# Values in front of the scores in the steady rounds of a window attention

## The chip, the cores and the metric

The kernel runs on one core of one Trainium2 chip. What counts is the time of one execution on the device in microseconds; the kernel before takes 2110.75 us, the median of three runs (2108.05 to 2111.23).

## What is computed

The input has 4 batches of 8 heads, 768 positions and a head dimension of 64. Each position attends to the 4 first positions of its sequence (the sinks) and to the 128 last ones (the window). The result, 3072 rows of 512, goes through 8 experts that are all applied, weighted by a gate that is normalised in 8 sweeps over rows and columns:

```python
keep = is_sink | in_window                 # n_sink = 4, window = 128
scores = np.where(keep, scale * q @ k.T, -1e9)
a = np.exp(scores - scores.max(-1)); a = a / (a.sum(-1) + 1e-09)
x = (a @ v)                                # rows of 8 heads x 64
logits = x @ w_gate                        # then exp, and 8 sweeps to P
out = sum(P[:, e:e+1] * (np.maximum(x @ w1[e], 0) @ w2[e]) for e in range(8))
```

## The kernel before

**Stages.** Attention comes first and takes the first 263 us of the span. The experts follow, in stages that are matmuls almost throughout. While attention runs, pieces of the first expert's products fill TensorE's time (`plain`, with the tiles g and o).

**Units and rounds.** A unit is one block of 128 queries of one batch and half of the heads (4 of 8): 4 batches x 6 blocks x 2 halves give 48 units, numbered n. The rounds are a software pipeline over the units. A steady round n (L868 to L935 in `steady_round`, n from 6 to 48) does, in the order of the code:

- it transposes queries and keys of unit n + 2 (L474 on VectorE, into KQ),
- it computes the scores of unit n + 1 (L502), one matmul for each of 4 heads, into the PSUM tiles st0 to st3,
- VectorE masks the scores and finds their extremes (L510), ScalarE takes the exponentials (L513): `soften`,
- it computes the values of unit n - 1 (L602): the attention weights PT times vr, and behind them the sinks' products (PS times VS),
- it does a piece of the expert's first product (L695) and one step of the gate's logits (L642),
- VectorE divides for unit n + 1 (L519, L520); ScalarE and VectorE finish the piece of the expert (L700, L701),
- TensorE transposes the weights of unit n (L543, into st1 and st2); VectorE copies one pair of heads to PT, ScalarE the other (both L549),
- `store_x` reads the values O of unit n - 1: ScalarE copies the share of a block that is begun (L619), VectorE adds the share that completes a block (L615),
- TensorE transposes the sinks' weights (L567, into st3), ScalarE copies them to PS (L569), and a piece of the expert's second product (L711) ends the round.

An attention window of 128 spans two blocks of keys, so the values of a unit go half to its own block and half to the one before; that is why a block is begun by one unit and completed by the next.

**What sets the order.** The steady rounds stand under a manual schedule: every engine issues in the order of the code. An engine takes its instructions in that order, and waits at one until the semaphores that it names have come.

**The tiles that matter.** O is the PSUM tile that the values write. It comes from a pool of two buffers that are taken in turn (`ps_o`), and the gate's logits (L640) are tiles of the same pool and name. So where a gate's tile was begun since the last O, the next O takes the buffer of the O just before it, which `store_x` read at the end of the last round. The tiles st0 to st3 serve scores, transposes and the sinks' transposes in turn.

Of the kernel before, what the change touches and what calls it, by code (L numbers as in the profile page):

```python
# [233 lines left out]
def tile_sink_attention_moe(ctx: ExitStack, tc: tile.TileContext, q, k, v, wg, w1, w2, out):  # L234

    nc = tc.nc
# [128 lines left out]
    def st_tile(shape, k=None):  # L365
        if k is None:
            k, turns[0] = turns[0] % 4, turns[0] + 1
        return ps_st.tile(shape, F32, name=f"st{k}")
# [96 lines left out]
    def transpose_qk(n):  # L465

        b, i, hh = units[n]
        us[n] = {}
        h0 = hh * HH
        t = KQ[hh]  # L470
        to = t[:, :, SINK:].rearrange("p r (a c) -> p r a c", a=2)[:, :, :, turn_of(b, i)]
        if n >= 2 * GB * FIRST:
            src = KS[n // (2 * GB)].rearrange("p (r a i t) -> p r a i t", r=HP, a=2, i=GB)[:, hh * NP:(hh + 1) * NP, :, i % GB]
            us[n]["high"] = nc.vector.transpose(to, src).ins  # L474
        else:
            pt = st_tile([P, 4, P], 3 if n == 1 else 0)
            for pr in range(NP):
                for j, nm in enumerate(("kr", "qr")):
                    nc.tensor.transpose(pt[:, 2 * pr + j, :], raws[nm, b, i][:, h0 + 2 * pr:h0 + 2 * pr + 2, :].rearrange("p h d -> p (h d)"), ident)
                    if n < 2 and (pr, j) in ((0, 0), (1, 1)) and (n, pr) != (0, 1):  # L480
                        spin(1, 5 - 2 * pr)
            us[n]["high"] = nc.scalar.copy(to, pt.rearrange("p (r a) t -> p r a t", a=2)).ins
        if i == 1:
            with nullcontext() if steady[0] else tc.issue_after(us[n]["high"]):
                nc.vector.tensor_copy(t[:, :, 0:SINK], t[:, :, place(b, 0)][:, :, 0:SINK])

    def scores(n, pr):

        b, i, hh = units[n]
        u = us[n]  # L490
        K, Q = KQ[hh][:, :, seen(b, i)], KQ[hh][:, :, CW:][:, :, turn_of(b, i)]
        if pr == 0:
            u["sc"] = att.tile([P, HH, CW], F32, name="sc", bufs=3)
            u["st"] = att.tile([P, 3, HH], F32, name="st", bufs=3)
            u["ps"] = {}
        hs = range(2 * pr, 2 * pr + 2)
        ps = {h: st_tile([P, K.shape[2]], h) for h in hs}
        u["ps"].update(ps)

        for h in hs:  # L500
            r0 = (h % 2) * D
            nc.tensor.matmul(ps[h], lhsT=Q[r0:r0 + D, pr, :], rhs=K[r0:r0 + D, pr, :], start=True, stop=True)  # L502
# [78 lines left out]
    def values(n):  # L581

        b, i, hh = units[n]
        u = us[n]
        keys, ready, _ = due_keys(n)
        if not keys:
            return
        O = u["O"] = ps_o.tile([P, NP, 2, P], F32, name="O")
        u["side"] = {q_: j for j, q_ in enumerate(sorted(keys[0][1], key=lambda q_: spot(keys[0][0], keys[0][1][q_])))}
        ops = []  # L590
        for pr in range(NP):
            for m, qs in keys:
                R = spots(PTR[hh][pr], [spot(m, s_) for s_ in qs.values()])
                sides = sorted(u["side"][q_] for q_ in qs)
                for h in range(2):
                    ops.append((O[h * D:(h + 1) * D, pr, sides[0]:sides[-1] + 1], raws[("vr", *units[m][:2])][:, hh * HH + 2 * pr + h, :], R[:, h]))
        for q_ in ready:
            if units[q_][1]:
                for pr in range(NP):
                    ops.append((O[:, pr, u["side"][q_]], seq[units[q_][0]][:, (hh * NP + pr) * P:(hh * NP + pr + 1) * P], us[q_]["PS"]))  # L600
        for j, (o_, x_, y_) in enumerate(ops):
            nc.tensor.matmul(o_, lhsT=x_, rhs=y_, start=(j < 2), stop=(j >= len(ops) - 2), skip_group_check=True)  # L602

    xrs = {}

# [196 lines left out]
    on = lambda j: 0 <= j < L  # L802
# [6 lines left out]
    def early_round(n):  # L809

        if units[n + 2][2] == 0:
            with (tc.high_priority() if n == -2 else nullcontext()):
                load_rows(("kr", "qr"), n // 2 + 1)
                if n < 2:
                    load_rows(("vr",), n // 2 + 1)
                elif n == 4:
                    load_rows(("vr",), n // 2)
            if units[n + 2][1] == 0:
                load_sinks(units[n + 2][0])
        squares_due(n)  # L820
        if n == -2:
            nc.sync.dma_start(wg_raw, wg.rearrange("(k p) e -> p k e", p=P))
            spread_sinks(0)
            split_sinks(0)
        if n == 0:
            spin(1, 4)
            scores(1, 0)
            soften(1, (0, 1))
            spin(1, 4)
            scores(1, 1)  # L830
            spin(1, 4)
            transpose_qk(2)
            with tc.issue_after(us[0]["divided"]), tc.issue_after(us[2]["high"]):
                soften(1, (2, 3))
            divide(1, range(HH))
        elif on(n + 1):
            for pr in range(NP):
                scores(n + 1, pr)
                soften(n + 1, range(2 * pr, 2 * pr + 2))
            divide(n + 1, range(HH))  # L840
        if on(n - 1):
            values(n - 1)
        if n >= START:
            run_fill(1)
        gate_step()
        for j in (0, 1) if n == -2 else (n + 2,) if n > 0 else ():
            transpose_qk(j)
        if on(n):
            transpose_p(n, 0)()
            if units[n][1]:  # L850
                gather_sinks(n)
        gate_step()
        if on(n):
            transpose_p(n, 1)()
        if on(n - 1):
            store_x(n - 1)
        gate_step()
        if on(n) and units[n][1]:
            transpose_sinks(n)
        if 0 < n < 3:  # L860
            spin(4 if n == 1 else 5, 5)
        if n >= START:
            run_fill(1)
# [4 lines left out]
    def steady_round(n):  # L868

        if n % 2 == 0:  # L870
            if on(n):
                load_rows(("vr",), n // 2)
            for j in (n // 2 + 1, n // 2 + 2) if n == STEADY else (n // 2 + 2,):
                if j < FIRST * GB:
                    load_rows(("kr", "qr"), j)
            if on(n + 2) and units[n + 2][1] == 0:
                load_sinks(units[n + 2][0])
        if n in ROWS:
            ROWS[n][0](ROWS[n][1])
        mid.extend(coming)  # L880
        coming.clear()
        behind[0] = False
        squares_due(n)
        turned = n + 2 < 2 * GB * FIRST
        if on(n + 2) and not turned:
            transpose_qk(n + 2)
        if on(n + 1):
            for pr in range(NP):
                scores(n + 1, pr)
        if on(n) and units[n][1]:  # L890
            gather_sinks(n)
        if on(n + 1):
            for h in range(HH):
                soften(n + 1, (h,))
        if on(n - 1):
            values(n - 1)
        run_fill(1)
        gate_step()
        flush(mid)
        behind[0] = True  # L900
        if on(n + 1):
            divide(n + 1, range(HH))
        flush(late)
        if turned:
            transpose_qk(n + 2)
        lows = [transpose_p(n, 0)] if on(n) else []
        gate_step()
        if on(n):
            lows.append(transpose_p(n, 1))
        flush(lows)  # L910
        if on(n - 1):
            store_x(n - 1)
        gate_step()
        if on(n) and units[n][1]:
            transpose_sinks(n)
        run_fill(1)
        flush(late)
        if n in PIECES:
            in_turn(*plain_tiles(*PIECES[n]))
        if n == L - 8:  # L920
            first_pieces.extend(pieces1(0))
        if n == L - 2:
            first_pieces.extend(pieces1(1))
        for _ in range({L - 8: 1, L - 6: 1, L - 4: 1, L - 3: 1, L - 2: 1, L - 1: 1, L: 2}.get(n, 0)):
            in_turn(*first_pieces.pop(0))
        flush(act_end)
        if on(n):
            b, i, hh = units[n]
            if (i, hh) == (0, 0):
                spread_sinks(b)  # L930
            elif (i, hh) == (0, 1):
                split_sinks(b)
        flush(pool_end)
        if L - 10 <= n < L - 2:
            sums1((n - (L - 10)) // 4, (n - (L - 10)) % 4)  # L935
# [785 lines left out]
```

## Time and profile before

| | |
|---|---|
| median of three runs | 2110.75 us |
| profiled execution | 2108.8 us |
| its span, first to last instruction | 2106.8 us |
| granted TensorE clock, mean | 0.999 |
| TensorE busy | 2087.2 us, 99% of the span |
| VectorE, ScalarE, GpSimd busy | 70%, 40%, 33% |
| steady rounds of attention | 37.8 to 263 us |

The times of the tables below count from the span's start. "PE" is TensorE's matmuls, "PEld" its weight loads, DVE is VectorE, ACT ScalarE. An fp32 matmul of the code stands in the trace as two, each with its weight load, so four scores are eight rows; and rows of one group that follow each other are merged, with their count behind an x. A matmul's end is modelled, so I go by the starts.

### The profile page before, as it was taken

What the parts mean: (1) busy time and instruction counts of PE and PEld (TensorE: products, weight loads), DVE (VectorE), ACT (ScalarE), POOL (GpSimd) and SP (SyncE); (2) the same over time, 40 slices, a digit from 0 to 9 for tenths busy, and PEclk for the clock granted to TensorE, in tenths of its full rate; (3) what the DMA queues carried; (4) which work ended last, traced back from release to release, by engine and by line L of the source; (5) the groups of instructions that cost most, each with busy time, mean ns of one, the idle gap of its engine ahead of it and who ended that gap; (6) DMA issues with size and microseconds to landing.
All of it is one profiled execution on the core that took longest, in us unless ns stands there. A gap on an engine that the chain in (4) does not pass through costs nothing.

```text
span 2106.8 us, 30678 instructions
## 1 busy us (share of the span) xinstructions
PE 2087.2 (99%) x10093; PEld 1708.5 (81%) x10093; DVE 1475.6 (70%) x2650; ACT 834.3 (40%) x1777; POOL 692.1 (33%) x854
## 2 busy tenths in 40 slices
PE   8999999999999999999999999999999999999998
PEld 6777778888888888888888888888888888888887
DVE  6777687777777766856766666666766666666666
ACT  6766625444444444433323233222433323233322
POOL 5654522233232331332232223223322232223223
PEclk9999999999999999999999999999999999999999
DMA  8656249989899996776666666668766666666662
GB/s 165 131 109 122 50 144 308 305 291 314 285 307 302 295 312 226 242 264 202 202 199 196 209 199 197 202 203 303 254 208 192 204 205 195 200 204 196 198 197 85
DMA packets 437269, 454.29 MB, mean 216 GB/s; under 512 B 139056, under 2 KB 305136, under 8 KB 436208
## 3 DMA queue, kind: packets, MB, share of 16 engines
q1 hardware_dynamic: 436184, 451.58, 69.4%
q8 instruction: 83, 1.36, 0.3%
q10 hardware_dynamic: 920, 0.68, 0.1%
q14 instruction: 82, 0.67, 0.1%
HBM read 314.69 MB, written 137.46 MB: 215 GB/s over the span
## 4 chain that ended last, share of the span: by engine, by line
PE 95%; DVE 1%; ACT 1%; DMA 1%; SPq 1%; POOL 1%; issue 0%; POOLq 0%; ACTq 0%; DVEq 0%
PE c L985 41%; PE o L1545 21%; PE held L1545 8%; PE o L1230 7%; PE held L1230 7%; PE O L602 2%; PE st L502 2%; PE st L543 2%; PE g L695 1%; PE o L711 1%; SPq L448 1%; PE O L642 1%; ACT sc L513 0%; DMA r<-in_moe_w_dram 0%; PE O L711 0%
## 5 line engine op out<-in xcount | busy, mean ns | idle before, releaser
L1011 ACT CAST hf<-w 128x512 fp32r<-128x512 f32 x448 | 265.1, 620 | 562.9 <-POOL w L1510 299.7
L1545 PE MATMUL o<-hf,W2q 128*128 128x512 f32 x1920 | 472.0, 389 | 0.0
L1545 PEld LDWEIGHTS o<-hf,W2q 128*128 128x128 f32 x1920 | 359.9, 188 | 75.5 <-DVE acc L1559 0.9
L985 PE MATMUL c<-T,W1q 128*128 128x512 f32 x1530 | 388.8, 389 | 0.2 <-DVE w L1491 0.2
L1012 DVE TENSOR_TENSOR hf<-w,hf 128x512 fp32r<-128x512 f32 x448 | 329.4, 764 | 76.3 <-ACT hf L1011 68.8
L985 PEld LDWEIGHTS c<-T,W1q 128*128 128x128 f32 x1530 | 286.8, 188 | 60.7 <-DVE w L1491 0.9
L1559 DVE TENSOR_TENSOR acc<-o,acc 128x512 f32<-128x512 f32 x298 | 204.7, 688 | 170.1 <-PE o L1545 170.0
L985 PE MATMUL c<-B,W1q 128*128 128x512 f32 x1134 | 278.3, 389 | 0.0
L985 PEld LDWEIGHTS c<-B,W1q 128*128 128x128 f32 x1134 | 212.6, 188 | 44.0
L1510 POOL TENSOR_TENSOR w<-w 128x512 f32<-128x512 f32 x64 | 82.6, 1291 | 493.2 <-DVE w L1492 493.2
L1491 DVE TENSOR_TENSOR w<-c,M 128x512 f32<-128x512 f32 x192 | 132.4, 689 | 137.9 <-PE c L985 133.6
L1487 ACT COPY M<-c 128x512 f32<-128x512 f32 x192 | 112.7, 587 | 249.6 <-PE c L985 249.5
L1545 PE MATMUL held<-hf,W2q 128*128 128x512 f32 x768 | 195.1, 389 | 0.6 <-DMA W2q<-w2s 0.6
L1230 PE MATMUL held<-W2f,h 128*128 128x512 f32 x672 | 171.1, 390 | 1.9 <-DVE W2f L1012 1.9
L985 PE MATMUL c<-T,W1f 128*128 128x512 f32 x672 | 170.9, 389 | 0.0
L1230 PE MATMUL o<-W2f,h 128*128 128x512 f32 x672 | 170.2, 389 | 0.0
L1545 PEld LDWEIGHTS held<-hf,W2q 128*128 128x128 f32 x768 | 143.9, 188 | 30.8 <-DMA W2q<-w2s 1.1
L1527 POOL TENSOR_TENSOR w<-w 128x512 f32<-128x512 f32 x64 | 106.2, 1659 | 176.2 <-DVE hf L1012 176.2
L1230 PEld LDWEIGHTS held<-W2f,h 128*128 128x128 f32 x672 | 125.8, 188 | 28.7 <-DVE W2f L1012 2.7
L1230 PEld LDWEIGHTS o<-W2f,h 128*128 128x128 f32 x672 | 126.1, 188 | 26.2
L985 PEld LDWEIGHTS c<-T,W1f 128*128 128x128 f32 x672 | 125.9, 188 | 26.4 <-issue 0.2
L1514 POOL TENSOR_TENSOR w<-w 128x512 f32<-128x512 f32 x64 | 83.8, 1309 | 175.9 <-DVE w L1492 171.7
(212 smaller groups left out, 2718.4 us busy)
## 6 DMA issues: line engine op xcount, KB each, us to landing
W2q<-w2s SPq DMA_DIRECT2D x448, 256.0 KB, 2.9
W1q<-w1s SPq DMA_DIRECT2D x444, 256.0 KB, 2.8
w1s<-W1f SPq DMA_DIRECT2D x56, 896.0 KB, 8.6
w2s<-WT SPq DMA_DIRECT2D x136, 256.0 KB, 4.2
r<-in_moe_w_dram SPq DMA_DIRECT2D x63, 512.0 KB, 4.5
w2s<-W2f SPq DMA_DIRECT2D x56, 256.0 KB, 5.8
PB<-psd SPq DMA_DIRECT2D x16, 512.0 KB, 3.7
w2s<-W2f SPq DMA_DIRECT2D x56, 128.0 KB, 6.2
```

What stands on the lines that cost most here:

```text
L502: nc.tensor.matmul(ps[h], lhsT=Q[r0:r0 + D, pr, :], rhs=K[r0:r0 + D, pr, :], start=True, stop=True)
L985: nc.tensor.matmul(ps, lhsT=w1(a, k), rhs=x[:, b, k, :], start=(start and j == 0), stop=(stop and j == len(TERMS) - 1), skip_group_check=n ...
L1011: nc.scalar.copy(dst[:, 0], src)
L1012: at(1, lambda: nc.vector.tensor_sub(dst[:, 1], src, f32(dst[:, 0])))
L1230: nc.tensor.matmul(o, lhsT=h[c, th][:, a, off:off + P], rhs=W2F[n][:, w, c, :], start=(begin and c == 0 and j == 0), stop=(end and c == 1 ...
L1487: nc.scalar.copy(t, T["c2"])
L1491: nc.vector.tensor_add(w, T["c1"], T[m])
L1510: nc.gpsimd.tensor_sub(S3, T["A11"], T["A21"])
L1514: nc.gpsimd.tensor_add(T["A21"], T["A21"], T["A22"])
L1527: at(k, lambda: nc.gpsimd.tensor_sub(T["A11"], w, T["A11"]))
L1545: nc.tensor.matmul(o, lhsT=W2Q[part, n, m][:, a, k * P:(k + 1) * P], rhs=F[part, n, H_OF[m]][:, w, :], start=(j == 0 and (begin or not hol ...
L1559: nc.vector.tensor_add(sums[m, k], o, sums[m, k])
```

## The change

In the steady rounds, `values` is called ahead of the scores, and no longer does the whole: it computes the windows' products and returns a function that does the sinks' products. That function is called behind the scores. In the first rounds (`early_round`) both parts follow each other as before. The bounds of the accumulation (start, stop) stay with the same products.

```diff
@@ values(n)
-            return
+            return lambda: None
...
+        windows = len(ops)
         for q_ in ready:
             if units[q_][1]:
                 for pr in range(NP):
                     ops.append((O[:, pr, u["side"][q_]], seq[units[q_][0]][:, (hh * NP + pr) * P:(hh * NP + pr + 1) * P], us[q_]["PS"]))
-        for j, (o_, x_, y_) in enumerate(ops):
-            nc.tensor.matmul(o_, lhsT=x_, rhs=y_, start=(j < 2), stop=(j >= len(ops) - 2), skip_group_check=True)
+        def run(span):
+            for j in span:
+                o_, x_, y_ = ops[j]
+                nc.tensor.matmul(o_, lhsT=x_, rhs=y_, start=(j < 2), stop=(j >= len(ops) - 2), skip_group_check=True)
+
+        run(range(windows))
+        return lambda: run(range(windows, len(ops)))
@@ early_round(n)
-            values(n - 1)
+            values(n - 1)()
@@ steady_round(n)
+        of_sinks = values(n - 1) if on(n - 1) else lambda: None
         if on(n + 1):
             for pr in range(NP):
                 scores(n + 1, pr)
+        of_sinks()
         if on(n) and units[n][1]:
             gather_sinks(n)
         if on(n + 1):
             for h in range(HH):
                 soften(n + 1, (h,))
-        if on(n - 1):
-            values(n - 1)
         run_fill(1)
```

From the added lines on, line numbers are up to six higher: the values stand at L605, the store's copy and add at L625 and L621.

The first place is on TensorE in the round that begins at 165.97 us in the trace of before. The st are the scores, KQ their operand; O is the values' tile, PT the weights, vr the values' input, PS and VS those of the sinks; g is the expert's first product. In brackets stand the engines whose semaphores a row waits for. Before:

```order
L502 MATMUL st_2526<-KQ_179 128x260 [waits Activation_49]
L502 MATMUL st_2527<-KQ_179 128x260 [waits Activation_49]
L602 MATMUL O<-PT_185,vr 64x256 [waits DVE_49]
L602 MATMUL O<-PT_185,vr 64x256
L602 MATMUL O<-PT_186,vr 64x256 x2
L602 MATMUL O<-PS,VS 128x128 x2
L695 MATMUL g_2470<-B_130,W_597 128x256 x2
```

The rows begin with the last two of the four scores; the values, which wait for VectorE, and the sinks follow. The same place in the changed kernel, from the values on:

```order
L605 MATMUL O<-PT_185,vr 64x256 [waits DVE_49,PE_49]
L605 MATMUL O<-PT_185,vr 64x256
L605 MATMUL O<-PT_186,vr 64x256 x2
L502 MATMUL st_2527<-KQ_179 128x260
L502 MATMUL st_2528<-KQ_179 128x260 [waits PE_49]
L502 MATMUL st_2531<-KQ_179 128x260 [waits PE_49]
L502 MATMUL st_2532<-KQ_179 128x260 [waits Activation_49]
L605 MATMUL O<-PS,VS 128x128 x2
L701 MATMUL g_2470<-B_130,W_597 128x256 x2
```

The values moved past the four scores, and the wait for VectorE moved with them to the head of the round; the sinks stayed behind. The second place is the next round, which begins at 171.06 us before. Before the change its scores and values are:

```order
L502 MATMUL st_2596<-KQ_175 128x260
L502 MATMUL st_2597<-KQ_175 128x260 [waits DVE_49]
L502 MATMUL st_2600<-KQ_175 128x260 [waits Activation_49]
L502 MATMUL st_2601<-KQ_175 128x260 [waits Activation_49]
L602 MATMUL O<-PT_183,vr 64x256 [waits DMAHW5_49]
L602 MATMUL O<-PT_183,vr 64x256
L602 MATMUL O<-PT_184,vr 64x256 x2
```

The second score waits for VectorE, the copy to PT that frees its PSUM tile, and the third for ScalarE's. After the change:

```order
L605 MATMUL O<-PT_183,vr 64x256 [waits DMAHW5_49,DVE_49]
L605 MATMUL O<-PT_183,vr 64x256
L605 MATMUL O<-PT_184,vr 64x256 [waits Activation_49]
L605 MATMUL O<-PT_184,vr 64x256
L502 MATMUL st_2601<-KQ_175 128x260
L502 MATMUL st_2602<-KQ_175 128x260 [waits PE_49]
```

The waits for the two copies moved from the scores to the values, the first of them to the round's first matmul. No row of VectorE, ScalarE, GpSimd or the DMA queues moves.

## Rows read from the trace of the kernel before

**Rows 1.** The page, part 4: shares of the chain that ended last.
```profile
PE 95%; DVE 1%; ACT 1%; DMA 1%; SPq 1%; POOL 1%; issue 0%; POOLq 0%; ACTq 0%; DVEq 0%
```

**Rows 2.** Busy time in a batch's twelve rounds: stretch, length, PE, PEld, DVE, ACT, POOL, clock, DMA.
```profile
165.97:227.72 61.75, 61.33 (x467) 46.15 (x467) 44.44 (x172) 40.79 (x145) 31.79 (x85) 1.00 0.57 115
```

**Rows 3.** TensorE's timeline, rounds A and B: start, us, engine, line, operation, count.
```profile
165.97 1.15 PE L502 MATMUL st<-KQ 64*128 64x260 f32 x8
167.05 1.08 PE L602 MATMUL O<-PT,vr 128*64 128x256 f32 x8
168.07 0.44 PE L602 MATMUL O<-PS,VS 96*128 96x128 f32 x2
...
171.06 1.15 PE L502 MATMUL st<-KQ 64*128 64x260 f32 x8
...
176.48 0.49 PE L502 MATMUL st<-KQ 64*128 64x260 f32 x2
```

**Rows 4.** Timeline of TensorE's weight loads in round A; in brackets the idle time before.
```profile
165.97 0.74 PEld L502 LDWEIGHTS st<-KQ 64*128 64x128 f32 x8 [0.36 <-issue]
167.05 0.63 PEld L602 LDWEIGHTS O<-PT,vr 128*64 128x64 f32 x8 [0.34 <-issue]
168.06 0.30 PEld L602 LDWEIGHTS O<-PS,VS 96*128 96x128 f32 x2 [0.39 <-issue]
```

**Rows 5.** VectorE's timeline in rounds A and B.
```profile
166.06 0.42 DVE L615 TENSOR_TENSOR xr<-O,xr 128x256 f32<-128x256 f32 x1 [0.87 <-ACT xr L619]
...
167.03 0.39 DVE L510 CUSTOM_DVE_ANT_0 sc<-st,mask 128x260 f32<-128x260 f32 x1
...
169.59 0.17 DVE L519 TENSOR_SCALAR st<-st 128x4 f32<-128x4 f32 x1
...
169.89 0.39 DVE L701 SCALAR_TENSOR_TENSOR h<-g,h 128x256 fp32r<-128x256 f32 x1
170.21 0.68 DVE L549 COPY PT<-st 128x512 f32<-128x512 f32 x1
...
175.14 0.66 DVE L549 COPY PT<-st 128x512 f32<-128x512 f32 x1
```

**Rows 6.** ScalarE's timeline in rounds A and B.
```profile
167.47 0.51 ACT L513 ACTIVATE sc<-sc,st 128x260 f32<-128x260 f32 x1 [1.28 <-DVE st L510]
...
169.38 0.19 ACT L513 ACTIVATION_READ_ACCUMULATOR sc<-sc,st 128x1 f32 x1
...
176.15 0.38 ACT L619 COPY xr<-O 128x256 f32<-128x256 f32 x1
```

**Rows 7.** First and last round like A: the scores' start, the store's add.
```profile
104.03 0.49 PE L502 MATMUL st<-KQ 64*128 64x260 f32 x2
104.07 0.42 DVE L615 TENSOR_TENSOR xr<-O,xr 128x256 f32<-128x256 f32 x1 [0.48 <-ACT xr L619]
...
248.72 1.15 PE L502 MATMUL st<-KQ 64*128 64x260 f32 x8
248.81 0.42 DVE L615 TENSOR_TENSOR xr<-O,xr 128x256 f32<-128x256 f32 x1 [0.77 <-ACT xr L619]
```

**Rows 8.** Weight loads, and VectorE's copy, at a batch's first blocks.
```profile
206.02 0.29 PEld L502 LDWEIGHTS st<-KQ 64*128 64x128 f32 x2 [0.36 <-issue]
206.26 0.39 DVE L549 COPY PT<-st 128x256 f32<-128x256 f32 x1
206.71 0.73 PEld L502 LDWEIGHTS st<-KQ 64*128 64x128 f32 x6 [0.39 <-DVE PT L549]
...
207.78 0.42 PEld L602 LDWEIGHTS O<-PT,vr 128*64 128x64 f32 x8 [0.34 <-DVE KQ L474]
```

**Rows 9.** A round whose first L510 waits for the scores.
```profile
222.06 1.40 PE L502 MATMUL st<-KQ 64*128 64x260 f32 x8
222.91 0.43 DVE L510 CUSTOM_DVE_ANT_0 sc<-st,mask 128x260 f32<-128x260 f32 x1 [0.31 <-PE st L502]
```

**Rows 10.** ScalarE's copies of O ahead of the round at 217.18 us.
```profile
216.79 0.65 ACT L619 COPY xr<-O 128x256 f32<-128x256 f32 x2
```

## Prediction

> **What bounds the kernel now.** I read the page first: the chain that ended last runs through TensorE for 95% of the span [rows 1]. What TensorE loses, the kernel loses, and no later stage can give it back. Then the stretches of attention: in the twelve rounds of one batch, 165.97 to 227.72, TensorE is busy 61.33 of 61.75 us, VectorE 44.44 and ScalarE 40.79 [rows 2]. So the other engines have room in sum, and the question is whether they are in time. For that I took the timeline of two rounds that follow each other, which I call A (165.97 to 171.06) and B (171.06 to 176.48), engine by engine [rows 3 to 6]. The reader is to see in it the order scores, values, sinks, then a piece of the expert's first product, the transposes, a piece of its second product, and the next scores at once.
>
> **What the change moves.** Only TensorE's order changes; VectorE, ScalarE, GpSimd and the DMA queues issue the same rows in the same order. No matmul is added or removed. Two things move in a round. The values stand 1.08 us earlier (the scores' length, 165.97 to 167.05 [rows 3]), and the scores 1.02 us later (the values' length, 167.05 to 168.07). The sinks stay where they are.
>
> *Changes of form.* Each of the three blocks begins after a gap of 0.34 to 0.39 us in the weight loads [rows 4], because the shape of the array that they use changes (64x128, 128x64, then full). Before, a round goes full, scores, values, full; now full, values, scores, full. Three changes either way, with gaps of like size: 0 us.
>
> *The values' new wait.* The values write O, a PSUM tile of a pool with two buffers, which the gate's logits share. In every round in which the gate took the other buffer, the new O is the one that the store of the round before reads last, with the VectorE add of L615. Before, the values stood behind the scores and this was hidden. In round A the add runs from 166.06 to 166.49 [rows 5]; TensorE is ready at 165.97 and would now stand still. A wait ends about 0.06 us after what it waits for: L549 ends at 206.65 and the loads behind it start at 206.71 [rows 8]. So the values start at 166.55, a loss of 0.58. Eleven rounds of this kind run from 104.03 to 248.72; in the first the add ends at 104.49 (0.46 late), in the last at 249.23 (0.51 late) [rows 7]. 11 x 0.57 = **6.3 us**, the 0.57 being 0.51 and the 0.06. Nothing of this is made up later, as the add hangs on a chain that TensorE itself starts: transposes, ScalarE's copies L549 and L619, then the add. Behind the waiting values stand the scores and all the rest of the round.
>
> Here the Trainium skill has a rule that would make the wait cheaper ("TensorE: Matmul & The Clock Gate", Part 3): weight loads may be pulled ahead of matmuls when they use other row groups, though matmuls keep their order. By it the scores' first loads, about 0.1 us (eight take 0.74 [rows 4]), could be done while the values wait, some 2 us less over 22 rounds. The trace shows a wait in which nothing behind it began: after two loads of scores at 206.02 the other six start together at 206.71, and the values' loads at 207.78 [rows 8]. I take 0 for it.
>
> *The scores are late, and what hangs on them.* In A the scores would start at 166.55 + 1.02 = 167.57 instead of 165.97. But VectorE did not take them at once before: it was at the transposing L474 and began the first L510 at 167.03 [rows 5]. Where VectorE does wait for the scores, L510 begins 0.85 after their start (222.06 to 222.91 [rows 9]). So here it begins at 168.42, 1.39 late. From there the old intervals hold: exponentials from 167.47, the last done at 169.56 [rows 6], VectorE's L519 at 169.59, L701 at 169.89, then the copy L549 from 170.21 to 170.89 [rows 5]. This copy waits for nobody at this place but stands in VectorE's queue behind the division. All of it comes 1.39 later, and the copy ends at 172.28. The next values read it, and B's would stand first at 171.06 + 0.58 = 171.64. They wait until 172.34, another 0.70. Before, only the second score of B needed this copy, and it was done 0.17 before the round began. What is late next: in B the division is followed by no L701, and the add of L615 again hangs on TensorE's transposes by way of ScalarE (L619 ends at 176.53 [rows 6]), so the next A loses 0.57 once more, with no growth. A pair of rounds takes 10.51 + 1.27 = 11.78 us.
>
> Eleven rounds follow an A. In six I take 0.70; in two (130.11 and 192.05), where the copy was late already and the scores waited for it, an estimated 0.45; in two with half as many values 0.70; in the last, at 253.80, which has no scores, 0.6. Together 4.2 + 0.9 + 1.4 + 0.6 = **7.1 us**.
>
> *The start of a batch's blocks* (206.02 and two like it). Here the scores wait already: from 206.02 to 207.78 they take 1.76 instead of 1.08, since the second one needs the copy that ends at 206.65 [rows 8]. The values' wait takes the place of that wait; by the same steps I estimate 0.3 more, 0.3 given back at a wait for GpSimd in the same round, and 0.5 in the next. In the third round O is freed by ScalarE's two copies at 217.44 against 217.18 [rows 10], 0.3; in the fourth the copy of L549 comes some 0.95 late, of which 0.25 was lost before. 1.5 x 3 = **4.5 us**. For the eight rounds before 82 us, of which one is like A, I take an estimate of **1.6 us**, between one A's 0.6 and half a microsecond a round, 4.
>
> *The sum.* 6.3 + 7.1 + 4.5 + 1.6 = 19.5 us. The profiled execution took 2108.8 (span 2106.8 and 2.0 around it), so 2128.3; the median of the runs is 2110.75, 2 us above it, and between the two I say **2129**. From below, only the direct waits: 6.3, the 0.3 and 0.3 at each batch's begin and 0.8 early, 9 in all, or 2118. From above, each of the 41 rounds with values and scores loses 0.70, as B does: 29 us, or 2138.
>
> **Rivals.**
> 1. *Only the wait for O counts.* The copy L549 is late, but something in VectorE's chain closes up. For it: VectorE is idle 0.87 us ahead of L615 [rows 5]. Against it: that idle time lies behind the copy, and the chain in front of it (four L510, four exponentials of 0.50, L519) has no gap to close. 2108.8 + 9 = 2118.
> 2. *The chain through VectorE and ScalarE bounds every round*, not only those behind an A, as every score is 1.02 late: 2138. For it: in A it ends just 0.17 before the next round. Against it: the copy in B ends at 175.80, 0.68 before the next round [rows 5].
> 3. *The values cover a wait that the scores had.* At 206.02 and its two likes the scores stood 0.68 for the copy L549; with values between, they never wait for their PSUM banks. This decides if O is free when TensorE arrives, that is if the add L615 ends half a microsecond sooner, or the values' wait turns out to belong to an older store. Then 3 x 0.68 = 2 us are gained: 2107. For it: before, no row charges the values with a wait for that add. Against it: there it stood hidden behind 1.08 us of scores, and the order of the changed kernel still names VectorE at the values, now first in the round.
> 4. *The change does less than it says*: the sinks' wait or the three changes of form cost nothing and the stall is taken back in the idle time of a later stage. The experts' stages have TensorE just as full, so I give it little: 2111.
>
> **How the numbers follow.** Forecast 0.64, first rival 0.14, second 0.13, third 0.05, fourth 0.04. The likeliest case has its own range from its unknowns (4.5 and 1.6, each between half and double): 2125 to 2135. To hold 8 in 10 the range reaches to the first rival and part of the way to the second: 2117 to 2140. What a measurement can tell from no change here is 0.2%, 4.2 us. The third and fourth rival lie within it, with 0.02 of the third beyond: faster 0.02, same 0.07, slower 0.91.
>
> **What would show it.** In the changed profile the values' weight loads should wait for VectorE, half a microsecond in every second round for the add of the store and in the round between for the copy of the transposed weights; the pairs of rounds should take 11.8 us instead of 10.5, and the expert stages should begin some 19 us later and last as long. If the rounds between wait for nothing, the second term was wrong; if the values begin with no wait, the first was, and the time would not rise.

## The result, and the profile after

The changed kernel takes 2127.17 us (median of 6 runs, 2124.87 to 2129.26), the kernel before 2108.07 (2107.36 to 2111.23) on the same chip: 1.0088 of its time, 95% interval 1.0077 to 1.0099, so some 19 us more. The prediction was 2129, with a range of 2117 to 2140. The profiled span is 2125.3 us (before 2106.8), the granted clock 0.999 in both.

The page's chain that ended last, shares by engine:

```profile
PE 91%; ACT 3%; DVE 3%; DMA 1%; SPq 1%; POOL 1%; issue 1%; DVEq 0%; ACTq 0%; POOLq 0%
```

TensorE had 95% of this chain [rows 1]; VectorE and ScalarE now stand in it with 3% each. The busy times of the same twelve rounds as in [rows 2] (stretch, length, PE, PEld, DVE, ACT, POOL, clock, DMA share, GB/s):

```profile
174.96:242.40 67.44, 60.85 (x466) 45.64 (x467) 43.75 (x173) 39.91 (x143) 31.95 (x85) 1.00 0.50 102
```

The twelve rounds take 67.44 instead of 61.75, 5.69 more, with the same work on TensorE (60.85 busy, 61.33 before): the difference is standing time. TensorE's timeline of the pair (start, us, engine, line, operation, count, in brackets the idle time before and who ended it) answers to [rows 3]:

```profile
174.97 1.08 PE L605 MATMUL O<-PT,vr 128*64 128x256 f32 x8 [0.58 <-DVE xr L621]
175.98 1.15 PE L502 MATMUL st<-KQ 64*128 64x260 f32 x8
177.06 0.44 PE L605 MATMUL O<-PS,VS 96*128 96x128 f32 x2
...
180.78 1.08 PE L605 MATMUL O<-PT,vr 128*64 128x256 f32 x8 [0.66 <-DVE PT L549]
181.79 1.15 PE L502 MATMUL st<-KQ 64*128 64x260 f32 x8
...
186.85 1.08 PE L605 MATMUL O<-PT,vr 128*64 128x256 f32 x8 [0.58 <-DVE xr L621]
```

The pair A and B takes 11.88 us (174.97 to 186.85) where it took 10.51. Values stand at the head of the round, scores behind, and two waits alternate: in A for the store's add (now L621), in B for VectorE's copy to PT. The weight loads of the pair, as in [rows 4]:

```profile
174.94 0.66 PEld L605 LDWEIGHTS O<-PT,vr 128*64 128x64 f32 x8 [0.99 <-issue]
175.98 0.74 PEld L502 LDWEIGHTS st<-KQ 64*128 64x128 f32 x8 [0.39 <-issue]
...
180.78 0.63 PEld L605 LDWEIGHTS O<-PT,vr 128*64 128x64 f32 x8 [1.09 <-DVE PT L549]
```

VectorE's and ScalarE's timelines, as in [rows 5] and [rows 6]:

```profile
174.40 0.42 DVE L621 TENSOR_TENSOR xr<-O,xr 128x256 f32<-128x256 f32 x1
...
176.83 0.43 DVE L510 CUSTOM_DVE_ANT_0 sc<-st,mask 128x260 f32<-128x260 f32 x1 [1.39 <-PE st L502]
...
179.43 0.17 DVE L519 TENSOR_SCALAR st<-st 128x4 f32<-128x4 f32 x1 [0.84 <-ACT sc L513]
...
180.04 0.68 DVE L549 COPY PT<-st 128x512 f32<-128x512 f32 x1
```
```profile
177.31 0.51 ACT L513 ACTIVATE sc<-sc,st 128x260 f32<-128x260 f32 x1 [2.78 <-DVE st L510]
...
179.22 0.18 ACT L513 ACTIVATION_READ_ACCUMULATOR sc<-sc,st 128x1 f32 x1
```

The idle 0.99 and 1.09 us ahead of the values' loads hold the wait and, as ahead of every block, some 0.4 us between loads; TensorE's rows above name who ended it. The add ends at 174.82, and the values' loads begin at 174.94. VectorE now waits 1.39 us for the scores; the exponentials, the division and the copy to PT follow behind, the copy ends at 180.72, and B's loads begin at 180.78. TensorE's waits in all of attention (who, for whom: us in total, times, longest):

```profile
PE O L605 <- DVE PT L549: 10.0, 15, 0.9
PE O L605 <- DVE xr L621: 9.0, 15, 0.7
PE O L605 <- ACT xr L625: 1.1, 4, 0.3
```

Together 20.1 us, where the kernel before has no such row. The experts' matmuls show that their stages give nothing back; the group of one of their lines, from before and from after (first to last start):

```profile
L985 PEld LDWEIGHTS c<-T,W1q x1530: 186/188/192, 868.5 to 2075.0; 128*128 128x128 f32 x192
```
```profile
L991 PEld LDWEIGHTS c<-T,W1q x1530: 186/188/192, 885.9 to 2092.6; 128*128 128x128 f32 x192
```

It starts 17.4 us later, ends 17.6 later, and lasts 1206.5 and 1206.7 us.

### The profile page after: what moved, and what is told of

It reads as the page before. It is cut to its first block, busy times and chain, and to the rows that moved or that the text cites. A ratio compares the mean times of both kernels' runs of the same rounds, so it can differ in the third digit from the quotient of the medians.

```text
span 2125.3 us, 30718 instructions
## 1 busy us (share of the span) xinstructions
PE 2086.7 (98%) x10093; PEld 1707.7 (80%) x10093; DVE 1472.1 (69%) x2650; ACT 832.5 (39%) x1777; POOL 694.0 (33%) x854
## 4 chain that ended last, share of the span: by engine, by line
PE 91%; ACT 3%; DVE 3%; DMA 1%; SPq 1%; POOL 1%; issue 1%; DVEq 0%; ACTq 0%; POOLq 0%
PE c L991 41%; PE o L1551 20%; PE held L1551 8%; PE o L1236 7%; PE held L1236 7%; ACT sc L513 2%; PE O L605 2%; PE st L502 1%; PE st L543 1%; PE g L701 1%; SPq L448 1%; DVE PT L549 0%; DVE sc L510 0%; PE O L717 0%; POOL sc L522 0%
## 5 line engine op out<-in xcount | busy, mean ns | idle before, releaser
L991 PE MATMUL c<-T,W1q 128*128 128x512 f32 x1530 | 388.8, 389 | 0.2 <-DVE w L1497 0.2
L991 PEld LDWEIGHTS c<-T,W1q 128*128 128x128 f32 x1530 | 286.8, 188 | 60.7 <-DVE w L1497 0.9
L991 PE MATMUL c<-B,W1q 128*128 128x512 f32 x1134 | 278.3, 389 | 0.0
L991 PEld LDWEIGHTS c<-B,W1q 128*128 128x128 f32 x1134 | 212.6, 188 | 44.0
L991 PE MATMUL c<-T,W1f 128*128 128x512 f32 x672 | 170.9, 389 | 0.0
L991 PEld LDWEIGHTS c<-T,W1f 128*128 128x128 f32 x672 | 125.9, 188 | 26.4 <-issue 0.2
```

Source lines behind the costliest of these rows:

```text
L991: nc.tensor.matmul(ps, lhsT=w1(a, k), rhs=x[:, b, k, :], start=(start and j == 0), stop=(stop and j == len(TERMS) - 1), skip_group_check=n ...
```

## The experiments

My theory: two waits on TensorE, for the add that reads O and for the copy to PT, make up the loss; the order itself costs nothing. The rivals: only one of the waits is real, the split of the sinks costs something of its own, or values ahead of scores bring a gain that the waits hide.

**1. The copy earlier.** VectorE's division, and the work behind it, moves behind the copies to PT:

```diff
-        if on(n + 1):
-            divide(n + 1, range(HH))
-        flush(late)
...
         flush(lows)
+        if on(n + 1):
+            divide(n + 1, range(HH))
+        flush(late)
```

> The changed kernel, with VectorE's division (and the expert's low part that follows it) moved behind the two copies to PT, so that the copy no longer stands behind the four exponentials. Theory of two waits: the values' waits for the copy (10.0 us in 15 rounds) go, the waits for the store's add (9.0) stay, 2127 - 10 = 2117. Rival, that the copy is late only because the wait for O has delayed the scores, or that ScalarE's copy or another wait takes its place: 2123 to 2127.

It took 2117.31 us (2115.06 to 2121.09), 1.0038 of before (1.0025 to 1.005). TensorE's waits:

```profile
PE O L605 <- DVE xr L621: 8.3, 15, 0.7
...
PE O L605 <- ACT xr L625: 1.2, 4, 0.4
```

The wait for the copy has no row any more; the wait for the add stays, 8.3 us in 15. The time falls by 9.9 us against the changed kernel, and its row there held 10.0. So the copy's wait is about half of the loss, and it comes from where the copy stands in VectorE's queue.

**2 and 3. O without the gate.** The gate's logits leave O's pool, so that O alternates between its two buffers. They go into a part of the expert's tile g (one tile for both), and add onto what lies there, so the gate's weights differ. Run 3 has the edit of run 1 as well.

```diff
-        lg = ps_o.tile([P, E], F32, name="O")
+        lg = shared[:, 256:256 + E]
...
-            nc.tensor.matmul(lg, lhsT=xr[:, kc, :], rhs=wg_raw[:, kc, :], start=(kc == 0), stop=(kc == KC - 1))
+            nc.tensor.matmul(lg, lhsT=xr[:, kc, :], rhs=wg_raw[:, kc, :], start=False, stop=True, skip_group_check=True)
...
+    shared = psg1.tile([P, 512], F32, name="g1")
+    bank1, bank2 = lambda shape: shared[:, 0:shape[1]], lambda shape: pso1.tile(shape, F32, name="o")
```

> The changed kernel, with the gate's logits taken out of the values' PSUM pool and put beside the expert's first product in its bank (the gate's sums are cut there, so the gate's weights differ; the work is the same), so that O has two buffers of its own. Theory of two waits: the waits for the store (9.0 and 1.1 us) go, those for the copy stay at 0.70 in the rounds that had them, since the scores are late by the values alone: 2127 - 10 = 2117. Rival, that the second wait only follows the first: 2108.

> Both edits together, logits apart (the gate's weights differ) and division behind the copies. Theory: neither wait is left and the scores' old waits are gone too, 2107 (between 2105 and 2110). If the order itself (changes of form, late scores) costs something, it remains here: with 0.1 us a round, 2111.

Run 2 took 2149.73 us (1.0181, 1.0164 to 1.0198), run 3 2142.70 (1.0171, 1.0142 to 1.02): slower than the kernel that they were to mend. TensorE's waits of run 2, then of run 3:

```profile
PE g L648 <- ACT h L706: 26.4, 18, 1.7
...
PE O L605 <- DVE PT L549: 0.6, 3, 0.2
```
```profile
PE g L648 <- ACT h L706: 26.5, 18, 1.7
```

The waits for the add and for ScalarE's copy did vanish, and in run 2 the wait for VectorE's copy, which the theory kept, fell from 10.0 to 0.6 us. But the edit brought a wait of its own: the logits write a tile that ScalarE's relu (L706) is still to read, and TensorE stands there 18 times, 1.5 us on average. That wait lies between scores and the next values and delays those values by itself, so the 0.6 us speak neither for nor against the rival. In run 2 the clock fell as well (columns as above, with the granted clock ahead of the DMA share):

```profile
178.00:189.00 11.00, 9.54 (x73) 6.87 (x72) 6.23 (x25) 7.27 (x26) 4.02 (x13) 1.00 0.54 103
189.50:192.50 3.00, 3.00 (x13) 1.86 (x13) 1.73 (x4) 1.54 (x4) 2.39 (x7) 0.50 0.05 14
```
```profile
188.40 0.39 PE L648 MATMUL g<-wg_raw,xr 128*128 128x8 f32 x2 [1.46 <-ACT h L706]
...
191.42 1.70 PE L605 MATMUL O<-PT,vr 128*64 128x256 f32 x8
```

After the wait of 1.46 us that ended at 188.40 the granted clock was 0.50 (1.2 GHz) from 189.50 on, and the same values took 1.70 us instead of 1.08. That happened in ten stretches of run 2, and in only four of run 3, which has the same 18 waits; the mean clock was 0.991 and 0.996. As a check, estimated from these rows: 2127.2, less the waits that went (9.0 + 1.1 + 9.4), plus 26.4, plus 17 for the clock (0.008 of 2150) gives 2151 for run 2. The same for run 3 gives 2127.2 - 20.1 + 26.5 + 6.4 = 2140. Both lie within 3 us of what was measured, but as tests of the two waits the runs are inconclusive: too much else moved.

**4. The sinks not split off.** The whole of the values stands ahead of the scores:

```diff
-        of_sinks = values(n - 1) if on(n - 1) else lambda: None
+        if on(n - 1):
+            values(n - 1)()
         if on(n + 1):
             for pr in range(NP):
                 scores(n + 1, pr)
-        of_sinks()
```

> The changed kernel with the sinks' products not split off: values and sinks both in front of the scores. A round then has four changes of the array's form instead of three, and the scores stand 0.28 us later. Theory, with some 0.15 us for a change of form: 40 x 0.15 = 6 us, and 0.4 in each of the 15 rounds that wait for the copy, 6 more: 2139. If a change of form costs nothing, the later scores alone: 15 x 0.28 = 4, 2131. If the split is what made the change slow: 2117 or less.

2137.11 us (2134.31 to 2138.39), 1.0126 (1.0109 to 1.0143). Waits, and TensorE's timeline:

```profile
PE O L605 <- DVE PT L549: 13.5, 16, 0.9
PE O L605 <- DVE xr L621: 10.2, 15, 0.9
...
PE O L605 <- ACT xr L625: 1.6, 4, 0.7
```
```profile
180.15 1.08 PE L605 MATMUL O<-PT,vr 128*64 128x256 f32 x8 [0.65 <-DVE xr L621]
181.16 0.44 PE L605 MATMUL O<-PS,VS 96*128 96x128 f32 x2
181.53 1.15 PE L502 MATMUL st<-KQ 64*128 64x260 f32 x8
...
186.33 1.08 PE L605 MATMUL O<-PT,vr 128*64 128x256 f32 x8 [0.89 <-DVE PT L549]
...
192.59 1.08 PE L605 MATMUL O<-PT,vr 128*64 128x256 f32 x8 [0.63 <-DVE xr L621]
```

9.9 us more than the change. The scores come one more block later, and the copy's wait grows with them, 0.66 to 0.89. So the split is not to blame; without it the change would cost more. The waits hold 25.3 us, 5.2 more than 20.1; the other 4.7 us, over 41 rounds with scores and values, are 0.11 a round. The trace has it without the noise of the medians: the pair takes 12.44 us (180.15 to 192.59) instead of 11.88, of which 0.30 are longer waits, so 0.13 a round remain. They stand at two places: the sinks, now behind the values, hold 0.37 us to the next start (181.16 to 181.53) instead of 0.28, and the expert's piece, now behind the scores, 0.81 instead of 0.76. In this order a round has one change of form more (values, sinks, scores, full), which the theory priced at 0.15, a figure that no row gave. But the scores behind the sinks begin after a gap of just 0.07 us in the weight loads, so a count of changes times a price is too coarse; that the shape is what costs the 0.13 is argued, not shown by itself.

**5. Both waits taken away by order.** As run 1, and in every second round the store (ScalarE's copy of O, then the add) goes between VectorE's and ScalarE's copies to PT, so that both come sooner:

```diff
+        early = n % 2 == 1
+        if early:
+            flush(lows[:1])
+            lows = lows[1:]
+            if on(n - 1):
+                store_x(n - 1)
         flush(lows)
+        if on(n + 1):
+            divide(n + 1, range(HH))
+        flush(late)
-        if on(n - 1):
+        if on(n - 1) and not early:
             store_x(n - 1)
```

> As e1 (division behind the copies to PT), and in the odd rounds, whose O the next values take over, the store of O stands between VectorE's copy and ScalarE's copy to PT, so that the add no longer hangs on ScalarE's copy. Theory of two waits: the wait for the add falls from 0.65 to some 0.1 or 0.2 in 15 rounds, 2117.3 - 7.5 = 2110 (2107 to 2112). If the wait for O has another cause than the lateness of the store: no change against e1, 2115 to 2117.

2107.64 us (median of 11, 2105.23 to 2110.68), against 2108.19 of before in the same rounds (21 runs): 0.9996, 0.9987 to 1.0005. All of the loss is gone. TensorE's timeline of the pair, VectorE's copy and add, and the longest of TensorE's waits:

```profile
165.92 1.08 PE L605 MATMUL O<-PT,vr 128*64 128x256 f32 x8
166.93 1.15 PE L502 MATMUL st<-KQ 64*128 64x260 f32 x8
...
171.01 1.08 PE L605 MATMUL O<-PT,vr 128*64 128x256 f32 x8
...
176.43 1.08 PE L605 MATMUL O<-PT,vr 128*64 128x256 f32 x8
```
```profile
169.87 0.69 DVE L549 COPY PT<-st 128x512 f32<-128x512 f32 x1 [0.32 <-PE st L543]
...
175.72 0.42 DVE L621 TENSOR_TENSOR xr<-O,xr 128x256 f32<-128x256 f32 x1
```
```profile
PE st L567 <- POOL SS L562: 2.3, 3, 0.9
```

The copy ends 0.45 us ahead of the values at 171.01, the add 0.29 ahead of those at 176.43; none of TensorE's rows has a bracket, and no wait of the values is left. The pair takes 10.51 us again, as before the change. Values ahead of scores thus cost nothing and bring nothing of their own, to within the 2 us that the interval leaves.

**6. The same two moves in the kernel before,** values behind scores.

> The kernel before (scores first, values and sinks behind them) with the same two moves on VectorE and ScalarE as e5. Theory: neither wait stands on TensorE's path there, and only the scores' own waits for the copy (1.2 us in 3 rounds) can go: 2107 to 2109. If the two moves gain by themselves, whatever TensorE's order, it is faster by as much as e5 is against the changed kernel: 2092.

2106.8 us, 0.9992 of before (0.9983 to 1.0002). With run 5 that makes four cells: the old order takes 2108 us without the two moves and 2107 with them, the new one 2127 without and 2108 with. The moves are worth 19.5 us to the one order and nothing that can be told to the other. No version here measurably beats the kernel before.

**7. The expert's piece between values and scores,** so that the scores come later still:

```diff
         of_sinks = values(n - 1) if on(n - 1) else lambda: None
+        run_fill(1)
         if on(n + 1):
...
-        run_fill(1)
         gate_step()
```

> The changed kernel with the piece of the expert's first product (0.76 us) moved from behind the sinks to between values and scores, so that the scores are later by 0.76 and nothing else is. One more change of form comes with it, 5 us by e4. Theory, that the wait for the copy is as long as the scores are late: 15 x 0.76 = 11 more, 2127 + 5 + 11 = 2143. Rival, that the copy is late for the wait for O alone: 2132.

2161.82 us (2158.45 to 2162.45), 1.0245 (1.0229 to 1.0261), 19 us more than I expected. Waits and timeline:

```profile
PE O L605 <- DVE PT L549: 17.7, 16, 1.2
PE O L605 <- DVE xr L621: 13.2, 15, 1.1
PE O L605 <- ACT xr L625: 2.6, 4, 1.0
PE st L543 <- DVE st L510: 2.6, 9, 0.3
```
```profile
190.06 1.08 PE L605 MATMUL O<-PT,vr 128*64 128x256 f32 x8 [1.19 <-DVE PT L549]
...
193.34 0.34 PE L648 MATMUL O<-wg_raw,xr 128*128 128x8 f32 x2
193.76 0.63 PE L543 MATMUL st<-ident,sc 128*128 128x128 f32 x4
...
196.87 1.08 PE L605 MATMUL O<-PT,vr 128*64 128x256 f32 x8 [0.89 <-DVE xr L621]
```
```profile
193.19 0.42 DVE L510 CUSTOM_DVE_ANT_0 sc<-st,mask 128x260 f32<-128x260 f32 x1
```

The direction is the theory's: scores later by a piece, a longer wait for the copy (0.66 to 1.19). But I had left the add's wait as it was, and it grew too (0.58 to 0.89): the store's copy on ScalarE now stands behind exponentials that are late, and the transposes wait for L510. These four rows hold 36.1 us, 16 more than the 20.1 of the change, and the time rose by 34.7. The list names only the longer waits, and the timeline has the most of the rest. The first transposes start 0.42 us behind the gate's matmuls (193.34 to 193.76) where the changed kernel has 0.14: they write a tile that VectorE's second L510 reads until 193.61. That is so 36 times and makes 12.4 us, of which 2.6 are in the list, so 9.8 more. The expert's piece, now behind the values, takes 0.90 us to the next start instead of 0.76, in 41 rounds 5.7 us. And from 62 to 69 us the granted clock was 0.51 in the mean, by estimate 3.4 us of lost time (0.49 of 7). Together 16 + 9.8 + 5.7 + 3.4 = 34.9, a balance and not a test of each term. Something else moved too, against my expectation: ScalarE's relu (L706) now stands ahead of the exponentials, though there it only fills time in which ScalarE was idle (2.59 us ahead of the one at 198.88).

## Why the prediction was right

**What bounds the kernel.** Right: TensorE stands 20.1 us at the values, the span is 18.5 longer (less than the waits, as others went, such as the scores' at a batch's start [rows 8]), and the experts last as long as before.

**Changes of form, 0 us.** The 0 is right for this change: run 5 has the new order without its waits and takes the old time, pair for pair. The reason given for it holds only in part. A gap of 0.34 to 0.39 us follows values and scores, but scores behind sinks or the expert's piece, which use the full shape, begin after only 0.07 and 0.13 in runs 4 and 7 (181.53 and 191.98); what the 0.36 ahead of the scores of before is, no run here shows.

**The values' new wait, 11 x 0.57 = 6.3 us.** The mechanism is in the trace, in the place and in the eleven rounds named (of the other 4 of the 15 waits for the add, three stand at a batch's start and one in the first steady rounds). The size came out a little low: the scores of A start at 175.98, and the loads 0.12 us behind the end of the add, where I had taken 0.06; a round loses 0.65, not 0.58. 11 x 0.65 = 7.2. B's loads, which wait for the copy, do begin 0.06 behind it. The values of A name two semaphores, VectorE's and TensorE's own; that this makes the 0.12 is argued only. The Trainium skill's rule ("TensorE: Matmul & The Clock Gate", Part 3), by which the scores' first loads could have been pulled ahead while the values wait, I had taken at 0, and the trace agrees with that: no load of L502 lies in the waits, and the eight start together at 175.98, behind a gap of 0.39. But these rows don't test the rule, which asks for other row groups: the values use all 128 rows of the array (128*64), so by its own condition it promised nothing here.

**The late scores, 7.1 us.** L510 begins 0.85 us behind the scores' start (176.83 and 175.98), as [rows 9] has it. The wait for the copy then costs B 0.72 where I had 0.70: the scores of the pair stood at 165.97, 171.06 and stand at 175.98, 181.79, so 10.01 and 10.73 late. One term of this step failed: the two rounds with half as many values. I charged each with 0.70; they lose nothing. TensorE's and VectorE's rows of one of them:

```profile
210.18 1.08 PE L605 MATMUL O<-PT,vr 128*64 128x256 f32 x8 [0.58 <-DVE xr L621]
211.19 0.71 PE L502 MATMUL st<-KQ 64*128 64x128 f32 x8
...
214.29 0.66 PE L605 MATMUL O<-PT,vr 128*64 128x128 f32 x8
214.88 1.19 PE L502 MATMUL st<-KQ 64*128 64x260 f32 x8
```
```profile
214.46 0.41 DVE L549 COPY PT<-st 128x256 f32<-128x256 f32 x1
```

The values at 214.29 start ahead of the copy at 214.46. They belong to the first block of a batch, and the code (`due_keys`, where i is 0) gives them only the keys of the block before, whose copy is two rounds older. I had carried the wait over from the pattern of the pair without asking which unit's PT these values read. That is 1.4 us of the sum. The rest: six rounds at 0.72, two at 0.45 (the round at 192.05 passes on 0.73 and the next gives 0.28 back), the last 0.73, of which 0.36 come back ahead of the experts, where TensorE stands 0.87 us for VectorE (L53) instead of 1.23, so 0.37: 5.6 us instead of 7.1. That nothing would be made up later was thus wrong by this 0.36.

**Batch starts and early rounds, 4.5 and 1.6 us.** The starts of the later two batches lose 1.2 us each by the shifts of the scores' starts, where I had 1.5; the first A's scores come at 108.52 instead of 104.03, and without the 1.02 of the values and the 0.65 of its wait that is 2.8, against 1.5 + 1.6. In all 5.2 instead of 6.1. The waits behind a batch's start are those named: at 230.48 for ScalarE's copies of O 0.29 (I had 0.3), at 236.35 for the copy to PT 0.93 (0.95).

**The sum.** 7.2 + 5.6 + 5.2 = 18.0, where the first matmul of the next experts (L985, now L991) comes 17.8 us later (290.20 and 308.02). Of the predicted 19.5 one term was 0.9 too low and two were together 2.4 too high. That the total came so close is in part luck, as these errors cancel in part.

**The rivals.** Only the wait for O (2118): refuted, the wait for the copy holds 10.0 us, and run 1, which takes it away, lands there at 2117. Every round bound by the chain (2138): refuted, the waits alternate: ahead of the next A the copy ends at 186.20, 0.62 before the values' loads. Values that cover the scores' wait (2107): with O and the copy in time there is still no gain to be told (run 5 against run 6). The change does less (2111): refuted.

## What to carry to other kernels

When an operation moves to the head of a loop's round, list for each of its operands and for its output buffer who finishes last, when, and how far that is from the round's start: what stood hidden behind the operation that was first is then paid in every round in which it is late. What is pushed back by the move starts its own chain later, and the price is the excess of that chain's end over the next round's start, not the push itself; here both were cured by reordering the queues of the other engines. Ask of each kind of round which buffer it reads: a round that looks like the others may read one that was ready rounds ago.

## What I had not expected of the hardware

A granted clock that falls within attention: in run 2, with its 18 waits of 1.5 us on average, it stood at 0.50 (1.2 GHz) for some 3.4 us at a time (once 6.8) in ten stretches, while the changed kernel with waits of 0.58 and 0.66 us kept 1.00 (the stretch 174.96 to 242.40). Run 3 has the same 18 waits and only four such stretches; what decides between them is open.
